# The second pair's up product taken from the unmixed rows: a gated recurrence followed by a low-rank mixer on one core

## The chip, the cores and the metric

The kernel runs on one core of one Trainium2 chip. The metric is the device time of one execution in microseconds. Smaller is better.

## The reference

The work has two stages. The first is a recurrence over 768 steps for 4 batches and 8 heads, with a 48 x 48 complex state that is scaled by a complex gate at each step. The second is a mixer over the sequence followed by a two-layer network over the channels (384 to 1536 to 384):

```python
mag = np.sqrt(a_re * a_re + a_im * a_im)
scale = np.minimum(mag, 0.999) / (mag + 1e-06)
a_re_n, a_im_n = (a_re * scale, a_im * scale)
for t in range(S):
    new_re = ar * S_re - ai * S_im
    new_im = ar * S_im + ai * S_re
    S_re, S_im = (new_re + kv, new_im)          # kv = k[t] (outer) v[t]
    y[:, :, t] = np.einsum('bhd,bhde->bhe', q[:, :, t], S_re)
...
h = x.transpose(0, 2, 1) @ U @ V                # x: y as (4, 768, 384), rank 32
u = x + h.transpose(0, 2, 1)
ch = np.maximum(u @ w_ch1, 0.0) @ w_ch2
return u + ch
```

## The kernel before

The sequence of each batch is cut into 6 chunks of 128 steps, 24 chunks in all. The recurrence is computed chunk by chunk in a parallel form. Per group of two chunks, `gates` works out magnitudes and angles on ACT and DVE (in the trace `gate`, `GL`, `GS`, `F`), with sums along the chunk on PE (`es ps`, `ph`). Per chunk, `prep` weights q and k (`qk`, `QKC`) and transposes them on PE (`tr`, L816; ACT copies the result to `QK`, L822). `chain` then forms the products within the chunk (`inner` L845, `y` L894 and L902) and the state that is carried on (`dk` L865), and leaves the chunk's rows x in a buffer `xo`.

The mixer works on pairs of chunks, `m` = 0 to 11, three pairs a batch. When all six chunks of a batch are there, three rank rounds (`rank`, L937) form r = U^T x. `spread` (L960) forms the mixing term V^T r for the two chunks of a pair (`mixed`), and DVE adds it to `xo` (L444). `turned` transposes the sum (`uTp`, L976) into `uT`. The up product multiplies `uT` by the first weight matrix `w1` (L991), ACT clips it at zero into `h`, and the down product (`down`) multiplies `h` by `w2`, after which DVE adds the result to `xo` and the rows are written out.

There are several forms of these products:

- Pair 0 (`m < AHEAD`) has its up product made ahead of the mix: `mixer(0, True)` transposes the unmixed rows and runs the up product on them, in two half pieces of 6 records each per two feature tiles, and ACT only copies the result. Once r is there, `ranked` multiplies it by `w1` (`rT`, L1005; `rw`, L1013), and `corrected` adds the share of the mix: twelve short products with 32 rows (`fix`, L1031, in four groups), which DVE adds to `h`, clipping at zero (L1037).
- Pair 1 has its up product made after the mix, 36 matmuls in six whole pieces of 12 records each.
- Pairs 2 to 11 use a form with fewer multiplications (`up_fewer`, `few`, L1103), from sums of weights that `combine` makes once and sums of the rows made by DVE (L1075).
- Pair 0 has a plain down product (`down` L1192); the others use `down_two` (L1235), again with fewer multiplications.

All matmuls are in fp32, and one such matmul shows as two records in the trace; a transpose shows as one.

Nothing is issued in the order of the code. Each step is recorded in a plan with the data that it reads and writes, and `Plan.order` issues the steps in the order of a list of numbers, `ORDER`, that was worked out beforehand. The list sets the place of each step on its own engine's queue, of loads on SP's queue as well. `SPARE` names steps ahead of which a few filler matmuls are put on PE; all of them lie in the first 40 us. The buffers for `h` of pair 0 (`hx`, in the area `extra`) and of the others (`h`) are different ones.

Of the kernel before, what the change touches and what calls it, by code (L numbers as in the profile page):

```python
# [114 lines left out]
)  # L115

SPARE = {
    125: 2, 135: 10, 199: 14, 209: 1, 223: 5, 243: 2,
}

DUMP = None
# [195 lines left out]
def kernel(  # L317
# [28 lines left out]
    FEWER, SINGLE, AHEAD = 2, 3, 1  # L346
# [1108 lines left out]
```

## Time and profile before

| | |
|---|---|
| median of 3 runs | 555.26 us (554.55 to 555.47) |
| the profiled execution | 554.71 us |
| its span, first to last instruction | 552.8 us |
| PE busy | 526.9 us |
| weight loads (PEld) busy | 477.3 us |
| DVE busy | 432.8 us |
| ACT busy | 317.8 us |
| moved by DMA | 39.92 MB |

PE is the matmul engine and PEld its weight loads, DVE the vector engine, ACT the scalar engine, POOL and SP the engines that mostly issue transfers. A row of a group or of the timeline gives line, engine, operation, and what is written from what; "x" and a number is the count of records. Since matmuls are pipelined, a record's own length is longer than its share of PE's time; the distance from one start to the next is the better price. A wait row gives the engine and the operation that waited, what it waited for, the total, the number of times and the longest, in us.

### The profile page before, as it was taken

To read this page: it belongs to the slowest core of one execution; us is meant where nothing else is said; L and a number is where in the kernel's file an instruction comes from. 1 tells how busy PE (TensorE), PEld (TensorE's weight loads), DVE (VectorE), ACT (ScalarE), POOL (GpSimd) and SP (SyncE) were. 2 spreads that over 40 slices of the span, in tenths; PEclk is the share of its full clock that TensorE was granted. 3 is DMA by queue.
4 is the path that set the end of the run, shared out by engine and by line. 5 is a ranking of instruction groups with operands and counts; after the bars stand their busy time and mean duration, and the time that the engine had idled before them with its cause. 6 is when DMAs were issued, how large, how long until landed. Compare 5 with 4: busy or idle time off the path is not lost.

```text
span 552.8 us, 16672 instructions
## 1 busy us (share of the span) xinstructions
PE 526.9 (95%) x7228; PEld 477.3 (86%) x7228; DVE 432.8 (78%) x828; ACT 317.8 (57%) x553; POOL 32.2 (6%) x61
## 2 busy tenths in 40 slices
PE   2899999999999999999999999999999999999996
PEld 1677776767999987999999998999999989999995
DVE  6899989999999987998787987786953635567352
ACT  6889999795597787567827956626512232110100
POOL 1000000001010000102001001002000000000000
PEclk9999999999999999999999999999999999999999
DMA  9988876523441354314513425003300000000001
GB/s 229 187 184 174 195 170 151 144 30 87 88 89 30 56 104 77 59 31 85 91 38 67 74 38 111 2 1 59 59 9 23 17 11 15 8 8 23 21 9 34
DMA packets 150688, 39.92 MB, mean 72 GB/s; under 512 B 145912, under 2 KB 147408, under 8 KB 150608
## 3 DMA queue, kind: packets, MB, share of 16 engines
q1 hardware_dynamic: 148400, 34.43, 31.2%
q0 software_dynamic: 2208, 4.35, 2.3%
q8 instruction: 59, 0.97, 0.7%
q14 instruction: 21, 0.17, 0.1%
HBM read 33.60 MB, written 4.76 MB: 69 GB/s over the span
## 4 chain that ended last, share of the span: by engine, by line
PE 73%; DVE 12%; ACT 4%; issue 2%; DMA 1%; POOL 0%; DVEq 0%; SPq 0%; ACTq 0%; POOLq 0%
PE down L1235 26%; PE few L1103 25%; PE tr L816 4%; PE dk L865 3%; PE inner L845 3%; PE y L902 3%; PE up L991 2%; PE y L894 2%; DVE xo L444 1%; ACT gate L438 1%; PE rank L937 1%; PE ph L755 1%; PE mixed L960 1%; PE uTp L976 1%; PE es ps L691 1%
## 5 line engine op out<-in xcount | busy, mean ns | idle before, releaser
L1111 ACT COPY h<-few 128x512 f32<-128x512 f32 x60 | 35.1, 585 | 87.3 <-PE few L1103 87.1
L1235 PE MATMUL down<-w,h 128*128 128x192 f32 x396 | 72.7, 330 | 0.9 <-DVE xo L444 0.7
L438 ACT ACTIVATE gate<-gate 128x768 f32<-128x768 f32 (+2 forms) x74 | 65.6, 900 | 9.2 <-DVE GS L750 3.8
L1235 PEld LDWEIGHTS down<-w,h 128*128 128x128 f32 x396 | 64.5, 190 | 3.7 <-issue 1.5
L822 ACT COPY QK<-tr 112x512 f32<-112x512 f32 x96 | 49.9, 596 | 17.8 <-PE tr L816 17.7
L444 DVE TENSOR_TENSOR xo<-down,xo 128x192 f32<-128x192 f32 (+1 forms) x79 | 29.9, 385 | 33.9 <-PE down L1235 33.4
L1115 DVE CUSTOM_DVE_ANT_1 h<-few,h 128x512 f32<-128x512 f32 x60 | 40.5, 686 | 15.7 <-PE few L1103 11.8
L1103 PE MATMUL few<-extra,w 128*128 128x128 f32 x400 | 50.9, 276 | 0.0
L1103 PEld LDWEIGHTS few<-extra,w 128*128 128x128 f32 x400 | 48.0, 192 | 0.1
L441 DVE TENSOR_TENSOR QKC<-qk,cs 128x768 f32<-128x768 f32 x48 | 44.4, 950 | 1.7 <-PE dk L865 1.3
L1235 PE MATMUL down<-stage 128*128 128x192 f32 x198 | 37.9, 330 | 0.4 <-DVE xo L444 0.4
L438 ACT ACTIVATE es<-es ps 128x384 f32<-128x384 f32 x48 | 20.1, 502 | 31.2 <-PE es ps L691 29.2
L444 DVE TENSOR_TENSOR h<-few,h 128x512 f32<-128x512 f32 x30 | 20.6, 688 | 20.4 <-ACT h L1111 12.1
L1179 POOL DMA_DIRECT2D out_dram<-xo x32 | 17.9, 558 | 313.8 <-DVE xo L444 297.7
L991 PE MATMUL up<-uT,w 128*128 128x256 f32 x144 | 34.5, 387 | 0.7 <-ACT uT L980 0.7
L1235 PEld LDWEIGHTS down<-stage 128*128 128x128 f32 x198 | 32.3, 190 | 1.7 <-DVE xo L444 1.0
L1103 PE MATMUL few<-gate,w 128*128 128x128 f32 x240 | 32.2, 278 | 0.4 <-DVE gate L1075 0.4
L435 ACT ACT_TABLE_LOAD x24 | 30.8, 1283 | 1.1 <-PEq L1439 0.7
L816 PEld LDWEIGHTS tr<-ident,QKC 64*112 64x112 f32 x768 | 24.2, 130 | 8.3 <-issue 3.6
L816 PE MATMUL tr<-ident,QKC 64*112 64x64 f32 x768 | 28.9, 221 | 2.4 <-DVE QKC L441 2.4
L991 PEld LDWEIGHTS up<-uT,w 128*128 128x128 f32 x144 | 26.4, 190 | 5.3 <-ACT uT L980 0.9
L1103 PEld LDWEIGHTS few<-gate,w 128*128 128x128 f32 x240 | 29.3, 192 | 0.8 <-PE uTp L976 0.6
(161 smaller groups left out, 1100.4 us busy)
## 6 DMA issues: line engine op xcount, KB each, us to landing
stage<-in_moe_w_ch_dram SPq DMA_DIRECT2D x12, 768.0 KB
gate<-in_a_im_dram SPq DMA_DIRECT2D x24, 192.0 KB
gate<-in_a_re_dram SPq DMA_DIRECT2D x24, 192.0 KB
VP<-in_v_dram SPq DMA_DIRECT2D x24, 192.0 KB
qk<-in_q_dram SPq DMA_DIRECT2D x24, 192.0 KB
qk<-in_k_dram SPq DMA_DIRECT2D x24, 192.0 KB
out_dram<-xo POOLq DMA_DIRECT2D x12, 192.0 KB, 2.2
out_dram<-xo POOLq DMA_DIRECT2D x20, 96.0 KB, 2.1
```

The lines of the kernel that those rows point to most:

```text
L435: ACT(1.4, rank, lambda: nc.scalar.preload_act_table_set(name), writes=[TABLE])
L438: return nc.scalar.activation(out=o, in_=i, func=f, **kw)
L441: nc.vector.tensor_tensor(out=o, in0=a, in1=b, op=OP.mult)
L444: nc.vector.tensor_tensor(out=o, in0=a, in1=b, op=OP.add)
L816: nc.tensor.transpose(out=get(*ps[r])[0:DQ, h], in_=get(*qkc)[at, h].rearrange("p u d -> p (u d)")[:, 0:DQ], identity=ident[at, at], tile_ ...
L822: nc.scalar.copy(out=get(*QK)[:, u].rearrange("p (h t) -> p h t", t=CH)[:, :, r * HC:(r + 1) * HC], in_=get(*ps[r])[0:DQ])
L991: nc.tensor.matmul(out=get(*ps)[:, e], lhsT=w1[:, f, (ff + e) * 128:(ff + e + 1) * 128], rhs=get(*uT)[:, f], start=(f == 0), stop=(f == KD ...
L1103: nc.tensor.matmul(out=get(*ps)[:, q], lhsT=w()[:, q * 128:(q + 1) * 128], rhs=v[0](), start=(n == 0 and q == 0), stop=True, skip_group_ch ...
L1111: ACT(c_act(n3 * CH) - 0.045, RU, lambda i=i, k=k: nc.scalar.copy(out=at(i, k), in_=get(*ps)), [ps], [o])
L1115: DVE(c_dve(n3 * CH), RU, lambda i=i, k=k: nc.vector._custom_dve(dve_ops.TENSOR_ADD_SAT, out=at(i, k), in0=get(*ps), in1=at(i, k), s0=math ...
L1179: queue.dma_start(out=out[b, c * CH:(c + 1) * CH, lo:hi], in_=get("xo", i)[:, lo:hi])
L1235: nc.tensor.matmul(out=get(*to)[:, part], lhsT=x(j), rhs=y[:, j], start=(first and j == 0), stop=(j == KH - 1), skip_group_check=not first)
```

## The change

`AHEAD` goes from 1 to 2: pair 1 is now treated as pair 0 was. Its rows are transposed unmixed, its up product is made from them in half pieces, and four groups of `fix` products with eight additions on DVE correct it once r and `rw` are there. The spreading and the mixing of its rows remain, since the sum is needed at the end, but the transposes no longer wait for it. `rw` is already made for pair 0 and is used again. Pair 1's `h` keeps its own buffer. The list `ORDER` is a new one with 18 more steps, and `SPARE` has 33 fillers in place of 34.

```diff
 SPARE = {
-    125: 2, 135: 10, 199: 14, 209: 1, 223: 5, 243: 2,
+    125: 4, 135: 10, 199: 12, 206: 3, 208: 4,
 }
...
-    FEWER, SINGLE, AHEAD = 2, 3, 1
+    FEWER, SINGLE, AHEAD = 2, 3, 2
...
         uT, h = ("uT", m), ("h", m)
         if ahead or m >= AHEAD:
             buffer(uT, "uT", 2, [128, KD, N])
-            if ahead:
+            if ahead and m == 0:
                 ring(h, "hx", [extra.rearrange("p (f t) -> p f t", t=N)])
             else:
                 buffer(h, "h", 1, [128, KF, N])
```

The list `ORDER`, before and after, is left out here; it is replaced as a whole.

169 rows, old and new, of the table ORDER are left out of this document.

## The prediction

> **What bounds the kernel now.** I read the page first, then the busy table by stage, then the waits of PE and of DVE, then single stretches of the timeline.
>
> ```profile
> span 552.8 us, 16672 instructions
> PE 526.9 (95%) x7228; PEld 477.3 (86%) x7228; DVE 432.8 (78%) x828; ACT 317.8 (57%) x553; POOL 32.2 (6%) x61
> PE 73%; DVE 12%; ACT 4%; issue 2%; DMA 1%; POOL 0%; DVEq 0%; SPq 0%; ACTq 0%; POOLq 0%
> ...
> 0.00:45.00 45.00, 29.69 (x464) 22.76 (x464) 38.96 (x78) 35.45 (x63) 2.17 (x14) 1.00 0.99 199
> 45.00:100.00 55.00, 53.49 (x922) 40.80 (x923) 51.57 (x86) 52.63 (x89) 0.00 (x0) 1.00 0.72 167
> 100.00:160.00 60.00, 59.11 (x609) 47.97 (x609) 59.41 (x101) 44.15 (x72) 5.07 (x7) 1.00 0.35 78
> 160.00:300.00 140.00, 137.82 (x2167) 129.54 (x2166) 123.56 (x242) 99.16 (x171) 10.99 (x17) 1.00 0.37 71
> 300.00:552.80 252.80, 246.82 (x3074) 236.24 (x3072) 159.30 (x325) 86.38 (x162) 13.93 (x23) 1.00 0.13 29
> ```
>
> The first lines give the span, the busy shares and the chain that ended last; PE holds 73% of that chain. The five rows are stages: after the stage's limits and its length come busy us of PE, PEld, DVE, ACT and POOL, then the granted clock (1.00 throughout), the DMA share and GB/s. Up to 45 us the DMA engines are full (0.99) and PE is only partly used. From 45 to 160 us PE, DVE and, up to 100, ACT are nearly full at the same time. From 160 us PE alone is full. So there is no stage after 45 us in which PE stands open for long. How long exactly, the waits say (total, times, longest):
>
> ```profile
> PE down L1235 <- DVE xo L444: 1.3, 4, 0.7
> PE ph L758 <- ACT gate L438: 0.8, 1, 0.8
> PE dk L865 <- issue: 0.8, 2, 0.5
> PE up L991 <- ACT uT L980: 0.7, 1, 0.7
> PE tr L816 <- DVE QKC L441: 0.5, 1, 0.5
> PE ph L755 <- PE tr L816: 0.4, 1, 0.4
> PE down L1192 <- ACT h L438: 0.4, 1, 0.4
> PE few L1103 <- DVE gate L1075: 0.4, 1, 0.4
> PE uTp L976 <- DVE xo L444: 0.3, 1, 0.3
> PE mixed L960 <- ACT r L943: 0.3, 1, 0.3
> PE down L1235 <- issue: 0.2, 1, 0.2
> ...
> DVE AT L848 <- PE inner L845: 2.0, 1, 2.0
> DVE F L764 <- ACT F L438: 1.5, 1, 1.5
> DVE GL L670 <- ACT GL L438: 0.9, 2, 0.6
> DVE gate L441 <- ACT gate L438: 0.8, 1, 0.8
> ```
>
> The PE rows are all waits of PE from 45 us to the end. They add up to 1.3+0.8+0.8+0.7+0.5+0.4+0.4+0.4+0.3+0.3+0.2 = 6.1 us. That is the whole stock that a better order, or work pulled forward, can fill after 45 us. The DVE rows are all its waits from 19.6 to 160 us: 5.2 us in 140. The kernel ends like this:
>
> ```profile
> 546.84 1.14 PE L1235 MATMUL down<-w,more 128*128 128x192 f32 x6
> 548.02 0.36 DVE L444 TENSOR_TENSOR xo<-down,xo 128x192 f32<-128x192 f32 x1 [0.42 <-PE down L1235]
> ```
>
> The last product ends at 548.0; one addition and the write of the output follow to 552.8. The change does not touch that tail of 4.8 us, so what counts is when PE comes to the end of its queue.
>
> **The change part by part.** The sum is made against the profiled execution, 554.71 us (span 552.8, with 1.9 us around it). The median of the three runs, 555.26, is 0.55 above it; I carry that 0.55 over.
>
> *The up product of pair 1 itself* removes nothing: 36 matmuls before, 36 after. It reads x instead of the mixed rows, so it may stand ahead of the rank rounds. The spreading and the mixing remain, since the sum xo is still wanted. The only possible gain is that matmuls are ready when PE would wait. I therefore looked at where the new order puts the twelve half pieces: one stands ahead of the last rank round, two more ahead of `rw`, three more ahead of pair 0's down products, four after these, two behind the transposes of chunk 6. In the old order eight of the twelve halves' worth stood ahead of the down products; now six do. So the product is freed from the mix, but PE does not get it earlier. Value: 0; the waits that it could fill are in the item on the order.
>
> *Twelve short products are added on PE* (four groups, 24 records). Pair 0's own show the price:
>
> ```profile
> 66.39 1.56 PE L991 MATMUL up<-uT,w 128*128 128x256 f32 x6
> 67.88 0.67 PE L902 MATMUL y<-G,QK 112*64 112x48 f32 x16
> ...
> 97.31 1.13 PE L1031 MATMUL fix<-V,more 32*128 32x256 f32 x8
> 98.37 0.62 PE L755 MATMUL ph<-GS,prefix_r 128*128 128x384 f32 x2
> ...
> 102.07 2.76 PE L991 MATMUL up<-uT,w 128*128 128x256 f32 x12
> 104.75 1.56 PE L1031 MATMUL fix<-V,more 32*128 32x256 f32 x16
> 106.25 2.86 PE L991 MATMUL up<-uT,w 128*128 128x256 f32 x12
> ```
>
> Columns: start, length, engine, line, operation, count of records. From start to the next start, 98.37-97.31 = 1.06 and 106.25-104.75 = 1.50, together 2.56 us for 24 records. A full-height record of the same width takes (104.75-102.07)/12 = 0.223 us. The lower bound is four at a time, 24 x 0.223/4 = 1.3; the upper, each group placed alone like the first (two such, 2.1, and the two small groups at half of it, 1.1), is 3.2. In the new order one small group stands beside pair 0's and the others apart, so I take 2.6. A gain is excluded here: PE has no wait of that size to hide them in. The Trainium skill (TensorEngine Tiling (Array Packing), Theoretical Speedup) gives up to 4x for 32 rows; by that the term would be an estimated 1.3 us, and the same page (Key Properties) says that a change of tiling drains the array. The measured 2.56 says that drains, or something like them, eat half the packing here; the sum goes by the 2.6.
>
> *The up product is cut in halves* (two operations of 6 records instead of one of 12). A half took 67.88-66.39 = 1.49, a whole 2.68, so a half between other kinds of work costs 1.49-1.34 = 0.15 more. Four of the twelve stand next to each other, eight apart: at most 1.2, at least 0, since the switch may be paid by a neighbour in either order. Taken: 0.3.
>
> *Eight corrections are added on DVE*, each with its addition and clipping:
>
> ```profile
> L1037 DVE CUSTOM_DVE_ANT_1 extra<-fix,extra x4: 681/684/685, 98.9 to 109.2; 128x512 f32<-128x512 f32 x4
> L1037 DVE CUSTOM_DVE_ANT_0 extra<-fix,extra x4: 411/414/418, 105.5 to 106.5; 128x256 f32<-128x256 f32 x4
> ```
>
> That is 4 x 0.684 + 4 x 0.414 = 4.4 us, on a queue that waits 5.2 us in the 140 us in which they must fit. On ACT the copies take the place of the clipping copies, one for one: 0. DVE's queue gets 4.4 longer and PE's 2.6+0.3 = 2.9, so DVE falls 1.5 us behind PE in the stretch up to 160 us. Queued behind these corrections on DVE are weighting and gates of the next chunks; who waits for those is PE, in the rows `down <- xo`, `tr <- QKC`, `few <- gate`, `uTp <- xo`. Bounds for new PE waits: 0 to 1.5. Taken 0.4, because PE holds other ready work, the down products, beside most of them.
>
> *The order is made anew*, on all queues, loads too (chunk 0's q and k now go ahead of the weight pieces). Loads can matter only while the DMA share is near 1, that is up to 45 us; the first up product waits for the first two chunks:
>
> ```profile
> 40.26 0.55 DVE L982 COPY uT<-uTp 128x384 f32<-128x384 f32 x1
> ...
> 45.03 4.15 PE L991 MATMUL up<-uT,w 128*128 128x256 f32 x18 [0.66 <-ACT uT L980]
> ```
>
> In the new order ACT's copy of that uT stands behind the same sum of ACT work. DVE's copy for chunk 0 stands some nine operations, about 4 us of DVE work, further back; it ran at 40.26, so this eats the reserve and no more. I take the same start, within 1 us. The filler matmuls (34 before, 33 after) all stand in the waits ahead of 40 us and cost nothing. After 45 us a new order can at best clear the 6.1 us and at worst add about half as much; both orders come from the same kind of planning, so I take -0.5 (bounds -6.1 and +3).
>
> Sum: 2.6 + 0.3 + 0.4 - 0.5 = +2.8 us: a profiled execution near 557.5 and, with the 0.55, **558.0 us**, 0.5% slower.
>
> **The rivals.**
>
> *A. The waits go (faster).* Freed from the mix, the up product of pair 1 is always ready and PE's waits vanish. For it: the waits for `ph`, `tr` and `mixed` that lie between 60 and 100 us lie where it can now stand. Against it: these are 0.8+0.5+0.3 = 1.6 us, and the new order puts only one half piece ahead of the last rank round. It decides once more than 2.9+1.1 = 4.0 of the 6.1 us go. With all gone but the issue rows (1.0 us): 555.26+2.9-5.1 = 553.1; with a start 1 us sooner, 552.1. This is the case on the other side.
>
> *B. PE is not the bound; the work is swallowed (no change).* PEld, the weight loads, are busy for 86%, and in the 45 to 100 us row for 40.80 of 55. If that open share were usable, 2.9 us would vanish in it: 555.3. The Trainium skill (Trainium Kernel Development and Optimization, Performance Expectations) says that matmul busy time is a bad measure of the distance to the limit and that busy weight loads are a good one; by it PE had about 14% to spare (an estimate from the 86%). These rows bear on it:
>
> ```profile
> L991 PEld LDWEIGHTS up<-uT,w x144: 186/190/192, 45.0 to 141.4; 128*128 128x128 f32 x144
> ...
> 350.00:360.00 10.00, 10.00 (x92) 10.00 (x91) 6.65 (x14) 4.54 (x9) 0.00 (x0) 1.00 0.00 0
> ```
>
> In the stretch at 45.03 eighteen up records run in 4.15 us without a wait, 0.23 each, and load weights for 0.190 each: 82% with nothing to spare. The narrower `few` records at 350 us load for 100%. So the open share belongs to wide operands, and the trace speaks against the rule here.
>
> *C. DVE becomes the bound up to 160 us (slower still).* If DVE's 4.4 us go fully into the chain and PE's 2.9 do not hide behind them because the two engines wait for each other in turn: 555.26+4.4+1.5 = 561.2. For it: DVE stands in the chain for 12%, and 59.41 of 60 us are busy. Against it: its waits of 5.2 us can take part of that.
>
> *D. It does not do what it says.* Excluded: the built program holds 24 short matmuls where 12 stood, and eight more clipping additions.
>
> **How the numbers follow.** Forecast (556.4 to 559.5): 0.47. A, beyond -0.2%: 0.23. B, and every balance within 0.2%: 0.13. C: 0.17. About 0.2%, 1.1 us, is what a measurement of this kernel can tell from none. So faster 0.23, same 0.13, slower 0.64. The range takes in A down to 552.0 and C up to 561.5; a start that moves more, or an order that adds its full 3 us on top of C, is left out.
>
> **What the profile after would show.** Right: 48 records on the `fix` line, together 5 us or a little more; PE's waits from 45 us still 4 to 8 us; the first `few` about 3 us later than before, and the same 3 us at the end; eight more corrections on DVE. Wrong towards A: the first `few` no later than before and PE's waits below 3 us, or the first up product well ahead of 45 us. Wrong towards C: waits of PE for DVE between 100 and 160 us that add up to over 2 us.

## The result, and the profile after

The changed kernel takes **558.42 us** (median of 20 runs, 556.97 to 561.57) against 555.55 us for the kernel before (20 runs, 554.44 to 557.82): a ratio of 1.0047, 95% interval 1.0035 to 1.0060, or +2.9 us. The prediction said 558.0. The profiled execution took 558.34 us, of which 556.5 are its span. Executions of one kernel differ by 1 to 2 us with their mean granted clock (the kernel before beside the first four experiments: 553.8 to 555.3 us at 0.998 or more, 555.6 to 556.4 us at 0.995 or 0.996), so that a difference below about 1 us is told from the medians and intervals, not from single profiles.

The page of the kernel after (span, busy time, chain that ended last; every line number is one higher than before):

```profile
span 556.5 us, 16728 instructions
PE 531.6 (96%) x7250; PEld 480.8 (86%) x7250; DVE 436.1 (78%) x836; ACT 318.9 (57%) x553; POOL 32.6 (6%) x61
PE 66%; DVE 16%; issue 7%; DMA 5%; ACT 5%; SPq 0%; DVEq 0%; POOLq 0%
```

PE has 4.7 us more and DVE 3.3 us more. PE's share of the chain fell from 73% to 66% and DVE's rose from 12% to 16%: a first hint that PE is not alone. The stages (limits, length, busy us of PE, PEld, DVE, ACT, POOL, granted clock, DMA share, GB/s):

```profile
45.00:100.00 55.00, 53.65 (x929) 41.89 (x927) 51.85 (x84) 52.49 (x89) 0.00 (x0) 1.00 0.76 174
100.00:160.00 60.00, 59.10 (x612) 46.43 (x609) 59.07 (x101) 41.91 (x69) 4.29 (x6) 1.00 0.35 71
160.00:300.00 140.00, 137.33 (x2155) 128.96 (x2154) 124.48 (x244) 100.32 (x171) 11.41 (x17) 1.00 0.35 66
```

From 100 to 160 us PE and DVE are both full, as they were before. The added work shows as a delay of what follows. The first `few` products, which stand behind all of the first two pairs' work, start at 163.2 us before and at 165.8 after; first the row of before, then that of after:

```profile
L1103 PE MATMUL few<-extra,w x400: 272/275/378, 163.2 to 528.1; 128*128 128x128 f32 x134
```

```profile
L1104 PE MATMUL few<-extra,w x400: 271/275/377, 165.8 to 531.8; 128*128 128x128 f32 x134
```

The delay is not complete there: the rank round of the second batch starts at 209.29 us before and at 213.08 after, 3.8 us later. One wait in between is that of a `few` product for DVE, 0.9 us at 171 us, where the kernel before has none.

The added steps themselves, and the waits of PE from 45 us to the end (total, times, longest), in the kernel after:

```profile
L1032 PE MATMUL fix<-V,more x48: 374/374/478, 102.0 to 144.1; 32*128 32x256 f32 x48
L1038 DVE CUSTOM_DVE_ANT_0 h<-fix,h x4: 417/422/430, 107.0 to 146.4; 128x256 f32<-128x256 f32 x4
L1038 DVE CUSTOM_DVE_ANT_1 h<-fix,h x4: 686/690/694, 135.1 to 146.7; 128x512 f32<-128x512 f32 x4
...
PE y L895 <- DVE AT L849: 1.4, 3, 0.9
PE ph L762 <- DVE F L765: 1.1, 1, 1.1
PE few L1104 <- DVE gate L1076: 0.9, 1, 0.9
PE up L992 <- ACT uT L981: 0.7, 1, 0.7
...
PE tr L817 <- DVE QKC L442: 0.2, 1, 0.2
```

The eleven wait rows add up to 5.9 us, against 6.1 before: nothing was filled on balance. The kernel ends as before, 3.7 us later:

```profile
550.57 1.14 PE L1236 MATMUL down<-w,more 128*128 128x192 f32 x6
...
551.74 0.36 DVE L445 TENSOR_TENSOR xo<-down,xo 128x192 f32<-128x192 f32 x1 [0.42 <-PE down L1236]
```

So time and outward signs came out as forecast. The experiments ask whether the reasons hold.

### The profile page after: what moved, and what is told of

It reads as the page before. It is cut to its first block, busy times and chain, and to the rows that moved or that the text cites. A ratio compares the mean times of both kernels' runs of the same rounds, so it can differ in the third digit from the quotient of the medians.

```text
span 556.5 us, 16728 instructions
## 1 busy us (share of the span) xinstructions
PE 531.6 (96%) x7250; PEld 480.8 (86%) x7250; DVE 436.1 (78%) x836; ACT 318.9 (57%) x553; POOL 32.6 (6%) x61
## 4 chain that ended last, share of the span: by engine, by line
PE 66%; DVE 16%; issue 7%; DMA 5%; ACT 5%; SPq 0%; DVEq 0%; POOLq 0%
PE down L1236 23%; PE few L1104 21%; DMA gate<-F 3%; PE up L992 3%; PE y L903 3%; PE dk L866 3%; PE tr L817 2%; PE inner L846 2%; PE y L895 2%; ACT gate L439 1%; PE mixed L961 1%; DMA gate<-in_a_im_dram 1%; PE uTp L977 1%; DVE qk L442 1%; PE rank L938 1%
```

## The experiments

**Theory 1** is that of the prediction: PE alone is the bound, so the short products cost their time on PE and DVE's additions next to nothing. **Rival 1**: the new order itself is what is worse, and would cost its 1.003 to 1.005 with the added work taken out as well. **Rival 2**: DVE's additions are the cost. Each ratio below is against runs of the kernel before on the same chip; the kernel after stands at 1.0047. The first four kernels are the changed one with one thing altered.

**no_fix** and **no_add** leave out pair 1's short products and additions, or the additions alone:

```diff
-                    for y in range(len(tiles[0][0])):
+                    for y in range(0 if m else len(tiles[0][0])):
...
-    lambda o=o, ps=ps: nc.vector._custom_dve(
+    lambda o=o, ps=ps: m or nc.vector._custom_dve(
```

The first edit, to the short products, is in no_fix alone, the second, to the additions, in both.

> The changed kernel without pair 1's four groups of short products and without their eight additions (pair 1 stays uncorrected and unclipped); order, halves and everything else stay. Theory 1 (the short products lie on a full PE queue and cost their start-to-start time, 3.3 us as the trace of after has it): about 555.2 us, ratio to before 0.998 to 1.001, the fix line back to 24 records and some 2.6 us. Rival 1 (the new order itself is what is worse): still 1.003 to 1.005. Rival 2 (the corrections on DVE cost it): the same as theory 1 here, told apart by the next run.

Measured: 560.13 us, 1.0090 (1.0068 to 1.0111). Less work, and slower than the full change: every expectation missed. PE's timeline and the windows around the place where two of the four groups had been:

```profile
141.67 0.67 PE L903 MATMUL y<-GM,QK 112*64 112x48 f32 x14 [0.66 <-ACT xo L914]
143.66 1.10 PE L895 MATMUL y<-VP,AT 64*64 64x48 f32 x32 [1.33 <-DVE AT L849]
...
140.00:144.00 4.00, 2.01 (x60) 1.76 (x59) 4.00 (x6) 3.64 (x6) 0.00 (x0) 0.90 0.66 130
144.00:148.00 4.00, 4.00 (x67) 3.82 (x61) 2.52 (x6) 3.46 (x5) 0.00 (x0) 0.50 0.36 71
148.00:152.00 4.00, 4.00 (x20) 4.00 (x20) 2.56 (x4) 2.33 (x6) 0.00 (x0) 0.75 0.20 40
```

Two things are to be seen. PE waits 0.66 and 1.33 us, the longer one for `AT`, which stands on a DVE that is busy for all 4.00 us. And the granted clock falls to 0.50, beginning before the second wait is over (1.00 up to 143.0 us, 0.71 in the next half microsecond). The clock column gives an estimate of the loss in this execution: (0.10+0.50+0.25) x 4 = 3.4 us. In the kernel after, the same place looks like this:

```profile
143.36 1.16 PE L1032 MATMUL fix<-V,more 32*128 32x256 f32 x12
144.75 0.68 PE L895 MATMUL y<-VP,AT 64*64 64x48 f32 x32 [0.23 <-DVE AT L849]
```

The 1.16 us of short products lie in that wait for DVE: with them 0.23 us of it is left, without them 1.33.

> The changed kernel with pair 1's short products but without their eight additions on DVE (pair 1 stays uncorrected and unclipped). DVE loses 4.4 us of work, PE none. Theory 1: PE's work stands, ratio 1.0035 to 1.005. Rival 2 (DVE is what bounds 100 to 160 us): 2 to 4 us less than after, ratio 0.998 to 1.001.

Measured: 556.77 us, 1.0032 (1.0020 to 1.0043). Between the two theories, and nearer to theory 1 (from 1.0035). By the ratios the additions are worth 0.8 us in this order, and the intervals overlap, so nothing at all is not excluded.

**fix_twice** and **add_twice** repeat pair 1's short products or its additions (`* (1 + m)` on the loop over y; `for _ in range(1 + m)` around the addition).

> The changed kernel with each of pair 1's twelve short products issued twice into the same place (the second overwrites the first): 24 more records on PE, nothing more on DVE. Theory 1: 1.3 us (four at a time) to 2.6 us (pair 0's price before) more than after, ratio 1.007 to 1.0095. Rival (PE has room, through waits or its weight loads): as after, 1.004 to 1.005.

Measured: 557.71 us, 1.0047 (1.0030 to 1.0064), the ratio of the kernel after. PE's timeline shows where the 24 records went:

```profile
143.79 2.11 PE L1032 MATMUL fix<-V,more 32*128 32x256 f32 x24
145.83 0.68 PE L895 MATMUL y<-VP,AT 64*64 64x48 f32 x32
```

Half of them stand where the rest of the wait for `AT` was, which is gone. By start-to-start times the 24 records take 1.9 us of PE's time in the three stretches together, and the profile lists no wait of PE between 100 and 160 us any more, where the kernel after has 0.8 us (0.4+0.2+0.2). So the records are not free on PE; about 1 us of them can be hidden, and the interval allows for another microsecond. Theory 1, with 1.3 to 2.6 us, fails here, though at its lower end only just.

> The changed kernel with each of pair 1's eight additions made twice on DVE (pair 1 is corrected by twice the amount): DVE gets another 4.4 us between 106 and 147 us, PE nothing. Theory 1: 0 to 0.7 us more than after, ratio 1.0045 to 1.006. Rival 2: 2 to 4.4 us more, ratio 1.008 to 1.0125.

Measured: 563.40 us, 1.0154 (1.0127 to 1.0180), 5.9 us above the kernel after by the ratios, more even than rival 2 expected. PE's waits from 100 to 165 us, and its clock:

```profile
PE down L1236 <- DVE h L1038: 2.7, 1, 2.7
...
152.00:156.00 4.00, 2.99 (x11) 3.00 (x12) 3.97 (x8) 2.19 (x6) 0.00 (x0) 0.68 0.00 0
156.00:160.00 4.00, 4.00 (x24) 4.00 (x24) 2.60 (x5) 0.52 (x1) 0.00 (x0) 0.89 0.48 96
```

The additions hold up the down product for 2.7 us, and the clock cut that follows costs an estimated (0.32+0.11) x 4 = 1.7 more. This execution also lost 1.7 us to a clock of 0.57 from 44 to 48 us, long before pair 1's additions, which begin at 107 us in the kernel after; that part is not the additions'. The one execution of the five with a mean clock of 1.000 took 561.8 us, about 3.9 us above the kernel after (1.0047 x 555.30 = 557.9), so in that execution DVE's work cost that much with next to no clock lost. From here on **theory 2**: PE and DVE share the bound up to 160 us, and a PE that waits for DVE for some 2 us can lose its clock as well.

**no_fix_filled** puts six filler matmuls into no_fix at the place of the wait (`SPARE` gets `748: 6`).

> As no_fix (pair 1 without its short products and additions), and with six filler matmuls on PE ahead of the operation for which PE waited 1.33 us at 142.3 us there. Theory 2 (the short products lie in PE's waits for DVE and cost nothing; without them PE stands idle for 2 us near 142 us, upon which its granted clock is halved for 6.7 us, 3.3 us lost): the clock stays at 1.00 from 140 to 152 us and the time falls by 2.5 to 3.4 us against no_fix, to a ratio of 1.002 to 1.0045. Rival (the cut has another cause than the idle time): the clock row stays near 0.50 behind 143 us and the time stays at 1.008 to 1.010.

Measured: 557.55 us, 1.0043 (1.0029 to 1.0056), below no_fix without overlap. The filler and the same windows:

```profile
141.95 1.58 PE L1388 MATMUL y<-ident 128*128 128x96 f32 x12
...
140.00:144.00 4.00, 3.39 (x82) 3.11 (x78) 4.00 (x6) 3.32 (x6) 0.00 (x0) 1.00 0.73 144
144.00:148.00 4.00, 4.00 (x61) 3.89 (x53) 2.52 (x6) 3.77 (x6) 0.00 (x0) 1.00 0.28 56
```

Work without any use on PE makes the kernel 2.6 us faster, and the clock stays at 1.00 in these windows. Over all executions the mean clock was 0.992 to 0.997 in no_fix and is 0.998 to 1.000 here. The Trainium skill (TensorE: Matmul & The Clock Gate, What's actually happening) says that the matmul clock is halved after an idle window of about 3.4 us, by windows that run freely. The halving agrees. The idle time that sufficed in no_fix was shorter, at most 2.0 us in two pieces.

The result also bears on rival 1: with pair 1's short products and additions gone, the time cannot be told from that of the kernel after (1.0047), just as rival 1 had it.

**old_order** is the change in the order of before: halves in a row at the old places, chunk 2's and 3's transposes ahead of their mixing, each group of short products behind its up product. **new_order** is the reverse, the kernel before in the new order, with pair 1's whole up products and transposes put back behind the mix. Both lists were mended by hand where the data demands it.

> The change with the order of before: both halves of each of pair 1's up products in a row where the whole stood, chunk 2's and 3's transposes moved ahead of their mixing, each group of short products with its additions behind its up product; all loads and all else as before. Theory 2a (what costs is DVE's 4.4 us and an order that has to make room for them): 1.004 to 1.009, since this order has no room made for them. Theory 1 (the price of the short products, 2.6 to 3.3 us): 1.0045 to 1.006. Rival 1 (the new order itself is worse): 0.999 to 1.002.

Measured: 565.35 us, 1.0189 (1.0171 to 1.0207).

> The kernel before with the new order, without the change: pair 1's up products whole and behind the mix, no short products and no additions for pair 1, its transposes put back behind the mixed additions; loads and all else as in the new order. Rival 1 (the new order itself is worse): 1.002 to 1.005. Theories 1 and 2 (order neutral): 0.998 to 1.002. Theory 2 with a PE idle time where the short products stood: up to 1.009, with a granted clock of about 0.5 for some 6 us between 130 and 160 us.

Measured: 565.29 us, 1.0188 (1.0171 to 1.0204). No theory had either number. In old_order (line numbers 14 lower than in the kernel after) DVE waits in its queue for short products that come late, and one wait of PE at 157 us is long:

```profile
DVE h L1023 <- PE fix L1017: 5.1, 3, 2.9
...
159.17 1.08 PE L1221 MATMUL down<-stage 128*128 128x192 f32 x5 [2.24 <-DVE xo L430]
...
156.00:160.00 4.00, 1.76 (x11) 1.47 (x10) 4.00 (x9) 2.81 (x8) 0.00 (x0) 1.00 0.49 98
160.00:164.00 4.00, 4.00 (x26) 3.85 (x25) 4.00 (x10) 2.21 (x5) 0.58 (x1) 1.00 0.01 2
```

The clock stays at 1.00 here after 2.24 us of waiting, where 2.0 us had been enough in no_fix. Windows that run freely, as that page has them, would give such a difference. The mean clock of old_order's five executions goes from 0.992 to 0.999, with 0.998 in the one shown, so the same kernel does not lose the same clock each time. In new_order PE waits along the mix, from 85 to 105 us:

```profile
PE uTp L962 <- DVE xo L430: 2.4, 2, 1.3
PE rT L991 <- ACT r L929: 0.8, 1, 0.8
PE fix L1017 <- ACT more L1003: 0.6, 1, 0.6
```

In the kernel after, pieces of pair 1's up product stand beside `rT` and `rw`, and PE has no wait between 85 and 100 us. So the freedom from the mix seems to be used by the new order; this is read from the places of the pieces, not shown by a run of its own. Since the hand-mended places bring waits of their own, new_order says nothing of the order's bare worth.

**old_order_2** mends those places: pair 1's groups with its additions are moved to where DVE should not have to wait for them. Of the 5.1 us of DVE's waits one of 1.5 us is left.

> As old_order (the change in the order of before), with the short products and additions of pair 1 put where DVE need not wait for them: in old_order DVE waited 5.1 us for short products that its queue held too early (2.9, 1.5 and 0.8). If those waits are what made old_order slow: 4 to 5 us less than it, 1.009 to 1.012. If DVE's 4.4 us have no room in this order at all: 1.015 to 1.019. If the new order is what costs (rival 1): at most 1.004.

Measured: 563.78 us, 1.0142 (1.0118 to 1.0166). By the ratio that is 7.9 us above the kernel before (8.7 by the medians), between the first two expectations, and its interval reaches into both. Four executions had a mean clock of 0.991 or 0.992 and took 563.4 to 564.3 us, two had 0.998 and took 560.7 and 561.2 us, so part of the cost is clock. All of them lie above the new order. For this work, then, the old order as mended by hand is no better than the new one. That answers only half of rival 1: whether the new order costs something by itself stays open, since no_fix_filled has its number.

**whole_up** makes pair 1's up products in whole pieces, at the later half's place (`((0,), (1,)) if ahead and m == 0 else ((0, 1),)`).

> The changed kernel with pair 1's up products in whole pieces (six of 12 records) at the place of the later half, all else the same. By the prediction's step (0.15 us for each half that stands alone): 0.3 to 1.2 us less than after, 1.0025 to 1.004. Rival (halves cost nothing): 1.004 to 1.006.

Measured: 560.01 us, 1.0084 (1.0070 to 1.0098). Both missed: whole pieces are 2.1 us slower. But this run moves six half pieces to later places as well, so it does not price the cutting alone. On PE the price is there: the half pieces of pair 1 at 134.38 and 139.20 us in the kernel after take 1.49 us each from start to next start, against 1.34 for half of a whole piece. The run suggests that the early places of the halves are worth more than that.

**before_fix_twice** and **before_add_twice** put the change's PE part and its DVE part separately into the kernel before, by repeating pair 0's short products or additions.

> The kernel before, pair 0's twelve short products issued twice into the same place (the second overwrites the first): 24 more records on PE between 97 and 106 us, nothing on DVE. If PE alone is the bound, as the prediction had it: 1.3 to 2.6 us more, ratio 1.0025 to 1.0045. If DVE shares the bound there (theory 2): 0 to 0.9 us, 1.000 to 1.0015, as fix_twice stood to after.

Measured: 556.16 us, 1.0022 (1.0011 to 1.0033): +1.1 us for 24 records. This lies between the two expectations, and its interval reaches into both. By start-to-start times the records take 2.2 us of PE's time (16 records 1.93 us where 8 took 1.06, and 32 records 2.79 where 16 took 1.50), so about half of that time is hidden; a wait of 0.43 us for ACT's copy of `h` is gone.

> The kernel before, pair 0's eight additions made twice on DVE (pair 0 is corrected by twice the amount): DVE gets 4.4 us more between 99 and 110 us, PE nothing; this is DVE's part of the change without the rest. If PE alone is the bound (the prediction: 0.4 us, at most 1.5): ratio 1.000 to 1.0027. If DVE shares the bound (theory 2): 2 to 4.4 us, 1.0035 to 1.008; more if PE stands idle long enough for its clock to be cut.

Measured: 560.92 us, 1.0113 (1.0095 to 1.0130): +5.9 us for 4.4 us of DVE work. The wait and the clock:

```profile
114.77 2.93 PE L1192 MATMUL down<-w,extra 128*128 128x384 f32 x4 [2.47 <-ACT h L438]
...
111.04 0.84 ACT L438 ACTIVATE GL<-GL 128x768 f32<-128x768 f32 x1 [2.16 <-DVE GL L654]
113.30 0.94 ACT L438 ACTIVATE gate<-GL,leps 128x768 f32<-128x768 f32 x1 [1.41 <-DVE gate L655]
114.14 0.58 ACT L438 ACTIVATE h<-up 128x512 f32<-128x512 f32 x1
...
112.00:116.00 4.00, 1.53 (x4) 0.84 (x3) 3.96 (x7) 2.70 (x4) 0.00 (x0) 0.79 0.01 2
116.00:120.00 4.00, 3.68 (x10) 1.55 (x9) 3.90 (x7) 4.00 (x7) 0.00 (x0) 0.78 0.00 0
```

PE waits 2.47 us for a copy by ACT. That copy stands behind `GL` and `gate` on ACT, for which ACT waited 2.16 and 1.41 us on a DVE that was busy throughout, with the additions among its work. In the kernel before these two waits are 0.2 and 0.7 us, and the same copy starts at 110.23 us, not at 114.14. So the lateness of DVE reaches PE over ACT. The clock cut costs an estimated (0.21+0.22) x 4 = 1.7 us. This is the plainest test of theory 1, and it fails by a factor of four against its upper bound of 1.5. The prediction's rows for PE's waits behind the corrections leave this way over ACT out.

**before_pool** tries to use the finding: six of `combine`'s sums, 0.68 us each, go from DVE to POOL in the kernel before (`(nc.gpsimd if n > 3 and k < 6 else nc.vector).tensor_tensor`).

> The kernel before with six of the thirteen sums that build pair 2's short weights (line 1156, 0.68 us each on DVE at 130 to 141 us) moved from DVE to POOL, which is idle there: DVE has 4.1 us less work, PE the same. Theory 2 (DVE shares the bound up to 160 us, 4.4 us more cost 5.9): PE's waits behind 130 us, 0.3+1.3 us in the trace of before, shrink: 0.5 to 1.6 us less, ratio 0.997 to 0.999. If DVE were no bound: 0.999 to 1.001. If POOL is much slower or slows DVE, and the sums come late for the third pair: above 1.001.

Measured: 559.68 us, 1.0079 (1.0052 to 1.0105), slower. POOL and DVE at that place, and a DVE row that stands beside POOL's last sum:

```profile
133.93 2.84 POOL L1160 TENSOR_TENSOR extra<-extra,w 128x512 f32<-128x512 f32 x2
136.84 2.28 POOL L1160 TENSOR_TENSOR extra<-w 128x512 f32<-128x512 f32 x1
140.43 1.59 POOL L1160 TENSOR_TENSOR extra<-w 128x512 f32<-128x512 f32 x1
...
133.61 4.38 DVE L1309 TENSOR_TENSOR w<-w 128x1152 f32<-128x1152 f32 x1
137.91 1.43 DVE L749 CAST GS<-gate 128x384 fp32r<-128x384 f32 x1
140.81 0.54 DVE L444 TENSOR_TENSOR G<-GM,dk 112x384 f32<-112x384 f32 x1
```

In the kernel before the same two operations read:

```profile
132.40 1.35 DVE L1305 TENSOR_TENSOR w<-w 128x1152 f32<-128x1152 f32 x1
...
L749 DVE CAST GS<-gate x18: 345/352/361, 96.4 to 388.4; 128x384 fp32r<-128x384 f32 x18
```

DVE lost 3.0 us on the first alone, and PE's wait for `AT`, which was to shrink, is 1.4 us long. The clock cut that followed in this execution (0.81, 0.50 and 0.83 from 144 to 156 us) came on top, and so did one from 25 to 35 us, ahead of the moved sums. The three executions with a mean clock of 0.998 or more took 557.4 to 558.5 us, still 2.4 to 3.6 us above the kernel before. The product with `dk`, one of whose inputs comes from the matmul results, kept its 0.54. The Trainium skill (SBUF — State Buffer, SBUF: two separate sides) states this: POOL and DVE hold a shared pair of ports in turn, each for a whole instruction, and only DVE's operations with two SBUF inputs or in a two-port mode are shut out. For the two products the trace agrees; that the cast `GS` ran in such a mode no row here shows.

## Why the time was right and the reasons were not

- **Start and end.** Right. The first up product starts at 44.73 us (45.03 before), the first `few` 2.6 us later and the end of the span 3.7 (about 3 forecast for both), the waits add up to 5.9 us (4 to 8 forecast), the `fix` line holds 48 records.
- **Short products, +2.6.** Right as PE time, wrong as kernel time. By start-to-start times the three stretches of the kernel after have 3.4, 1.1 and 1.2 us, 5.6 together, 3.1 more than the 2.56 before. But PE was not full of its own work: as many records again cost 1.1 us in the kernel before and nothing that can be measured in the kernel after. "A gain is excluded here: PE has no wait of that size" failed, because it set the products against single waits of the old trace and not against the waits for DVE that the rest of the change would make.
- **Halves, +0.3.** As PE time the 0.15 for each half stands in the trace. What it is in the kernel's time no run shows; whole pieces, put at the later half's place, cost 2.1 us more.
- **DVE, +0.4 (at most 1.5).** The size that no_add gives in the new order, 0.8 us, lies within the bounds; a second helping of the same additions cost 5.9 us there (add_twice), so the order has room for little more than the first. The reason does not hold: in the kernel before, as much DVE work at pair 0's place cost 5.9 us. DVE's waits of 5.2 us in 140 were set against the additions; those waits lie ahead of single steps and are no room for eight additions, and a late DVE stops ACT and PE long enough to cost clock.
- **Order, -0.5 (-6.1 to +3).** Not measured alone. Against the old order it is worth more than -0.5: the two parts measured there sum to 1.1+5.9 = 7.0 us, and the whole change in it, placed by hand, cost 7.9 by the ratio, against 2.9 in the new order. That makes an estimate of 4 to 5 us, which takes hand-made places for the old order's best. In the other direction, the new order with pair 1's short products and additions gone still stands at 1.0043, 2.4 us above the kernel before.
- **Sum.** 2.6+0.3+0.4-0.5 came out at 2.8, close to 2.9, but that is luck. By the runs in the new order the short products and additions hold some 1 us of it, not 3.0 (2.6+0.4), and the rest would lie in the order and the halves, not -0.2 (0.3-0.5). By those in the old order the additions are far dearer and the order makes up for it. Either way errors of about 2 us or more cancel.
- **Rivals.** C had the right mechanism for the old order, DVE as a bound beside PE, and its 561.2 us would not have been far off there (old_order_2: 560.7 to 564.3). In the new order the additions do not cost that, and C's sign in the trace, over 2 us of waits for DVE between 100 and 160 us, is absent (0.2+0.4 us); at one such place the short products lie in the wait. B, swallowed work, holds in part for the short products, through waits; that it was the weight loads no run shows. A did not happen.

What stays open is how the remaining 2.9 us divide. Without the additions 1.0032 is left, without additions and short products 1.0043 with fillers in their place; both lie above 1. Either the order is good only with the work that it was planned for, or it, with the halves, is itself the larger part of the cost. A new order planned for the reduced work would tell; it was not tried. The group of pair 1 that stands in pair 0's stretch (28 records in 3.4 us, where 24 took 2.56) may wait for a result buffer that DVE frees; that was not tried either.

## What to carry to other kernels

Where two engines are both nearly full in a stage (59 of 60 us here), ask what each added microsecond costs on each of them by doubling an existing step there, before trusting the one that holds most of the chain. Added work and the order made for it have to be priced together: the same change costs 2.9 us in an order made for it and 7.9 in the old one with places found by hand. A step that lies in another's wait can be nearly free, and taking it out can cost more than it did. A sum that comes out right does not show that its terms are.

## What the runs showed of the hardware

- Two waits of PE of 0.66 and 1.33 us within 2.7 us were enough for a granted clock of 0.50 (no_fix), at an estimated cost of 3.4 us; with 1.58 us of filler matmuls in that place the clock stayed at 1.00 (no_fix_filled). A wait of 2.24 us elsewhere passed without a cut (old_order).
- A sum of 128x512 on POOL took 1.3 to 2.3 us against 0.68 on DVE, and DVE's `w<-w` beside it went from 1.35 to 4.38 us (before_pool).
